# Block transposes for the softmax maxima, and two quads of heads in one accumulator, in a decode kernel that reads a KV cache

## The chip, the cores and the metric

The kernel runs on one core of one Trainium2 chip. The metric is the device time of one execution in microseconds, the median of several runs. Before the change it is 721.58 us (3 runs, 721.48 to 721.66).

## The reference

One decode step for two batch rows: attention over a cache of 4096 keys with 32 heads, a GELU MLP, and a gate that mixes the two. All values are float32.

```python
x (2,1,576); k_cache, v_cache (2,32,4096,128); wq (576,4096); wo (4096,576); w1 (576,4608); w2 (4608,576)
g = sigmoid((x * gate_w).sum(-1, keepdims=True))
q = (x @ wq) as (2,32,1,128)
p = softmax(einsum("bhqd,bhkd->bhqk", q, k_cache) * 128**-0.5)
a = einsum("bhqk,bhkd->bhqd", p, v_cache) reshaped to (2,1,4096) @ wo
b = gelu(x @ w1 + b1) @ w2 + b2
out = g * a + (1 - g) * b
```

## The kernel before

**Loads.** One large tile, `ring`, has three slots of 128 x 16384 numbers (8.39 MB). SyncE's queue fills them in a fixed order: first wq and w1, then K and V of 16 quads (a quad is four heads of one batch row: head e has partitions 32e to 32e+31, 128 keys each), and at last, in three loads, w2 and wo. `load_next` issues the next load into a slot as soon as what was in it has been used. The last load holds wo's rows 16 to 31, in pieces that get smaller (16-23, 23-27, 27-30, 30-31, then row 31 in three parts).

**One quad.** VectorE multiplies K by q in place (`mul`, L508), GpSimd adds two halves of a part of it (L512), VectorE sums (`red`, L513 and L514) into 128 scores a partition. `max_p` (L518) takes each partition's maximum. `max_t` (L523) is a TensorE matmul: the 128 maxima, broadcast to 128 columns, against a diagonal matrix `idsc` that holds the softmax scale, so that PSUM has all maxima in every row. `max_n` (L527) takes the negated maximum of each head's 32 columns. `softmax` (L533) runs four exponentials on ScalarE into `p`, one for each head, with the sums in `rs`. `av` (L544) multiplies p, 32 columns at a time, with V: each group of 16 columns (4 heads x 4 key blocks) is followed by the next group's 16, so half of the 32 rows that come out are of no use. `keep` (L556) masks the accumulator on VectorE, and `combine` (L562) adds the useful rows into the accumulator `oall`.

**Order.** The order on every engine is that of the program, written by hand. In iteration i of the loop over quads stand `max_n` and `softmax` of quad i-1, `mul` and `red` of quad i, `av` of quad i-1, `max_p` and `max_t` of quad i, then `keep` and `combine` of quad i-1. Every fourth iteration `q_unit` makes the next four quads' q.

**The end.** After the last K, `mlp_out(0, 24)` multiplies w2's first rows (L369 is the matmul of all rows that go to the accumulator `acc`, two to a row, and each of float32 is done in two passes), then come the last `av`, `keep`, `combine`, the normalisation (`norm_sum`, `norm_t`, `o_turn`) between further w2 rows, and `wo_out(0, FOLD)`. `last_out` copies `acc` with ScalarE (L448), takes the rows of wo from FOLD on into a second accumulator `res` (L459, four matmuls to a row, L483 for part of row 31), adds the copy with a fold matmul (L469) behind row FOLD + 3, copies `res` out of PSUM (L479, L488) and writes the result (L489).

Of the kernel before, what the change touches and what calls it, by code (L numbers as in the profile page):

```python
# [8 lines left out]
F32 = mybir.dt.float32  # L9
AF = mybir.ActivationFunctionType  # L10
ALU = mybir.AluOpType
AX = mybir.AxisListType
P = 128
# [6 lines left out]
def kernel(  # L20
# [14 lines left out]
    nc = tc.nc  # L35
# [6 lines left out]
    E = 4  # L42
    N = B * H // E
    PE_ = P // E
    R = E * SK // P
    RB = 512 // DH
    NT = R // RB
# [15 lines left out]
    SCALE = float(DH) ** -0.5  # L63
# [4 lines left out]
        (("w2", 28, 36), ("wx", 0, 1), ("wo", 0, 8), ("wo", 8, 16)),  # L68
        (("wo", 16, 23), ("wo", 23, 27), ("wo", 27, 30), ("wo", 30, 31), ("wo", 31, 32)),
    )  # L70
    FOLD = 23
    SLOT = R * DH
    ALIGN = 512
    FREE0 = 16512
# [5 lines left out]
    rp = ctx.enter_context(tc.tile_pool(name="rp", bufs=1))  # L80
    cp = ctx.enter_context(tc.tile_pool(name="cp", bufs=1))
    qm = ctx.enter_context(tc.tile_pool(name="qm", bufs=1))
    qp = ctx.enter_context(tc.tile_pool(name="qp", bufs=2))
    sp = ctx.enter_context(tc.tile_pool(name="sp", bufs=2))
    ep = ctx.enter_context(tc.tile_pool(name="ep", bufs=1))
    ps_acc = ctx.enter_context(tc.tile_pool(name="ps_acc", bufs=1, space=bass.MemoryType.PSUM))
    ps_av = ctx.enter_context(tc.tile_pool(name="ps_av", bufs=2, space=bass.MemoryType.PSUM))
    ps_big = ctx.enter_context(tc.tile_pool(name="ps_big", bufs=1, space=bass.MemoryType.PSUM))
    ps_o = ctx.enter_context(tc.tile_pool(name="ps_o", bufs=1, space=bass.MemoryType.PSUM))
    ps_sm = ctx.enter_context(tc.tile_pool(name="ps_sm", bufs=3, space=bass.MemoryType.PSUM))  # L90
# [80 lines left out]
    def temp(n, parts=P):  # L171
        t = ring[:parts, used["t"]:used["t"] + n]
        used["t"] += n
        assert used["t"] <= SLOTS * SLOT
        return t

    def late(n, parts=P):
        t = ring[:parts, used["e"]:used["e"] + n]
        used["e"] += n
        assert not seq and used["e"] <= used["z"]  # L180
        return t
# [18 lines left out]
    def load_next(what):  # L200

        free.add(what)
        while seq and held[-SLOTS] in free:
            load()
# [24 lines left out]
    ident = cp.tile([P, P], F32, name="ident")  # L229
    make_identity(nc, ident)  # L230
    ones = cp.tile([P, 1], F32, name="ones")
    nc.gpsimd.memset(ones, 1.0)
    idsc = cp.tile([P, P], F32, name="idsc")
    nc.scalar.mul(idsc, ident, SCALE)


    NPB = 1
    NQ = 4
    EB = E * RB
    NO = N * E  # L240
    pt = []
    for j in range(NPB):
        t = cp.tile([P, NT * EB + 32 - EB], F32, name=f"p{j}")
        nc.gpsimd.memset(t, 0.0)
        pt.append(t)
    rs = cp.tile([P, NO], F32, name="rs")
    nc.gpsimd.memset(rs, 0.0)


    sel = ident.rearrange("p (j c) -> p j c", j=4)[:, :, :EB].rearrange("p j (e r) -> p j e r", e=E)  # L250
    selr = cp.tile([P, RB], F32, name="selr")
    nc.vector.tensor_reduce(selr, sel.rearrange("p j e r -> p r j e"), AX.XY, ALU.add)
    pick = cp.tile([P, 2 * NO - E], F32, name="pick")
    nc.vector.memset(pick, 0.0)
    nc.vector.tensor_reduce(pick[:, NO - E:NO], sel.rearrange("p j e r -> p e j r"), AX.XY, ALU.add)

# [69 lines left out]
    qps2 = ps_sm.tile([NO, DH], F32, tag="sm", name="qps2")  # L328
    for f in range(HG):
        nc.tensor.matmul(qps2, to[:, f], qrow[:, f * DH:(f + 1) * DH], start=(f == 0), stop=(f == HG - 1))  # L330
    qall = cp.tile([NO, DH], F32, name="qall")
    nc.scalar.copy(qall, qps2)  # L332


    mine = cp.tile([NO, N], F32, name="mine")
# [64 lines left out]
    t = temp(NF * B).rearrange("p (r b) -> p r b", b=B)  # L400
# [18 lines left out]
    def mlp_x():  # L419
        for s in range(XS):  # L420
            acc_mm(hx[:, s], rows["wx"][:, s], s, lo=1)
# [23 lines left out]
    def last_out():  # L445
        res = ps_big.tile([32 * (NC - 1) + B, DO], F32, tag="big", name="res")
        sums = late(DS)
        nc.scalar.copy(sums, acc)  # L448

        def half(t, s):  # L450
            if s < 2:
                return t[:, s * DO:(s + 1) * DO]
            return t.rearrange("p (q g c) -> p g q c", q=2, g=2)[:, s - 2]

        def cols(row, s):
            return half(row[:, s // 2 * DS:(s // 2 + 1) * DS], s)

        def part(r, s):
            nc.tensor.matmul(  # L459
                res[32 * s:32 * s + B], oP[:, :, r], cols(rows["wo", r], s),  # L460
                start=r == FOLD, stop=r == 31, skip_group_check=True,
            )

        for r in range(FOLD, 31):
            for s in range(NC):
                part(r, s)
            if r == FOLD + 3:
                for s in range(NC):
                    nc.tensor.matmul(  # L469
                        res[32 * s:32 * s + B], fold[:, s // 2], half(sums, s),  # L470
                        start=False, stop=False, skip_group_check=True,
                    )

        osb = late(D, B)
        cpy = (nc.vector.tensor_copy, nc.scalar.copy)
        for s in range(2):
            part(31, s)
        for s in range(2):
            cpy[s](osb[:, s * DO:(s + 1) * DO], res[32 * s:32 * s + B])  # L479
        DW = DO // 2  # L480
        for q in range(2):
            for s in range(2, NC):
                nc.tensor.matmul(  # L483
                    res[32 * s:32 * s + B, q * DW:(q + 1) * DW], oP[:, :, 31], cols(rows["wo", 31], s)[:, q],
                    start=False, stop=True, skip_group_check=True,
                )
        for s in range(2, NC):
            cpy[s - 2](cols(osb, s), res[32 * s:32 * s + B].rearrange("p (q c) -> p q c", q=2))  # L488
        nc.sync.dma_start(out.rearrange("b s d -> (b s) d"), osb)  # L489


    st, mx, mt, bias, avs = {}, {}, {}, {}, {}
    oT = cp.tile([P, B, H], F32, name="oT")

    oall = ps_o.tile([NO, 512], F32, name="oall")
# [11 lines left out]
    def mul(i):  # L507
        nc.vector.tensor_mul(kt[i], kt[i], qs[i].unsqueeze(1).to_broadcast([P, R, DH]))  # L508

    def red(i):  # L510
        t = kt[i][:, :HALVED]
        nc.gpsimd.tensor_add(t[:, :, :DH2], t[:, :, :DH2], t[:, :, DH2:])  # L512
        nc.vector.tensor_reduce(st[i][:, HALVED:], kt[i][:, HALVED:], AX.X, ALU.add)  # L513
        nc.vector.tensor_reduce(st[i][:, :HALVED], t[:, :, :DH2], AX.X, ALU.add)  # L514

    def max_p(i):
        mx[i] = sp.tile([P, 1], F32, tag="m", name=f"m{i}")
        nc.vector.tensor_reduce(mx[i], st[i], AX.X, ALU.max)  # L518


    def max_t(i):
        mt[i] = ps_sm.tile([P, P], F32, tag="sm", name=f"mt{i}")
        nc.tensor.matmul(mt[i], mx[i].to_broadcast([P, P]), idsc, start=True, stop=True)  # L523

    def max_n(i):
        bias[i] = sp.tile([P, E], F32, tag="bs", name=f"bs{i}")
        nc.vector.tensor_reduce(bias[i], mt[i].rearrange("o (e p) -> o e p", e=E), AX.X, ALU.max, negate=True)  # L527

    def softmax(i):
        p = pt[i % NPB][:, :NT * EB].rearrange("p (t c) -> p t c", c=EB)  # L530
        for e in range(E):
            w = slice(e * PE_, (e + 1) * PE_)
            nc.scalar.activation(  # L533
                p[w, :, e * RB:(e + 1) * RB], st[i][w].rearrange("p (t c) -> p t c", c=RB), AF.Exp,
                bias=bias[i][w, e:e + 1], scale=SCALE, accum_out=rs[w, i * E + e:i * E + e + 1],
            )


    def av(i):
        ps = ps_av.tile([P, 512], F32, tag="av", name=f"av{i}")  # L540
        p = pt[i % NPB]
        for t in range(NT):
            j = t % 4
            nc.tensor.matmul(  # L544
                ps[32 * j:32 * j + 32],
                p[:, EB * t:EB * t + 32],
                vt[i][:, RB * t:RB * (t + 1)].rearrange("p r d -> p (r d)"),
                start=(t < 4),
                stop=(t >= NT - 4),
            )  # L550
        avs[i] = ps


    def keep(i):
        t = ep.tile([P, RB, DH], F32, tag="avs", name=f"avs{i}")
        nc.vector.tensor_mul(  # L556
            t, avs[i].rearrange("p (r d) -> p r d", d=DH), selr.unsqueeze(2).to_broadcast([P, RB, DH])
        )
        avs[i] = t

    def combine(i):
        nc.tensor.matmul(  # L562
            oall, pick[:, NO - E - i * E:2 * NO - E - i * E], avs[i].rearrange("p r d -> p (r d)"),
            start=(i == 0), stop=(i == N - 1), skip_group_check=True,
        )


# [16 lines left out]
    for i in range(N):  # L584
        k = i - 1
        if 0 <= k:
            max_n(k)
            softmax(k)
        st[i] = sp.tile([P, R], F32, tag="s", name=f"s{i}")
        mul(i)  # L590
        red(i)
        if 0 <= k:
            av(k)
            load_next(("v", k))
        if (i + 1) % NQ == 0 and i + 1 < N:
            q_unit((i + 1) // NQ)
        load_next(("k", i))
        max_p(i)
        max_t(i)
        if 0 <= k:  # L600
            keep(k)
            combine(k)

    k = N - 1
    max_n(k)
    softmax(k)
    mlp_out(0, 24)
    av(k)
    load_next(("v", k))
    assert not seq  # L610
    keep(k)
    combine(k)
    turn = late(P)
    nc.vector.tensor_copy(turn.rearrange("p (h k) -> p k h", k=KB), ident.rearrange("p (k h) -> p k h", k=KB))
    osum = late(DH, NO)
# [6 lines left out]
    mlp_x()  # L622
    wo_out(0, FOLD)
    last_out()


# [26 lines left out]
```

## Time and profile before

| | |
|---|---|
| median of the runs | 721.58 us |
| span of the profiled execution, first to last instruction | 719.8 us |
| time of that execution outside its span | not shown; the median is 1.8 us above the span |
| read from HBM | 308.59 MB |
| instructions | 3981, of them 1695 matmuls and 1695 weight loads on TensorE |
| busy: TensorE, VectorE, ScalarE, GpSimd | 237.2, 516.8, 38.3, 143.8 us |
| granted TensorE clock, mean over the span | 0.663 |

How to read it: PE is TensorE's matmuls, PEld its weight loads, DVE VectorE, ACT ScalarE, POOL GpSimd, SP SyncE; a name with q (SPq) is that engine's sequencer. A row of a group gives line, engine, operation, output <- inputs, shapes, count, then busy time and the mean in ns of one, and then the idle time of the engine just before, with what ended it. A row in order of time starts with start and duration in us; where it merges several instructions the duration is from the first to the last or their busy time, and the idle time before is in brackets. L and a number is a line of the kernel.

### The profile page before, as it was taken

To read this page: it belongs to the slowest core of one execution; us is meant where nothing else is said; L and a number is where in the kernel's file an instruction comes from. 1 tells how busy PE (TensorE), PEld (TensorE's weight loads), DVE (VectorE), ACT (ScalarE), POOL (GpSimd) and SP (SyncE) were. 2 spreads that over 40 slices of the span, in tenths; PEclk is the share of its full clock that TensorE was granted. 3 is DMA by queue.
4 is the path that set the end of the run, shared out by engine and by line. 5 is a ranking of instruction groups with operands and counts; after the bars stand their busy time and mean duration, and the time that the engine had idled before them with its cause. 6 is when DMAs were issued, how large, how long until landed. Compare 5 with 4: busy or idle time off the path is not lost.

```text
span 719.8 us, 3981 instructions
## 1 busy us (share of the span) xinstructions
PE 237.2 (33%) x1695; PEld 72.1 (10%) x1695; DVE 516.8 (72%) x146; ACT 38.3 (5%) x143; POOL 143.8 (20%) x31
## 2 busy tenths in 40 slices
PE   0682022230516060504142140506060503224198
PEld 0330000010101010101010010101010101001033
DVE  0104969789695969596969879696969596978900
ACT  0010010100001010101010100101010101010000
POOL 1000130404050403022040404040503113040400
PEclk9986557575757565755757575757575665757589
DMA  9999999999999999999999999999999999999997
GB/s 409 412 443 431 433 441 419 455 416 448 426 444 427 426 438 430 437 430 441 434 433 433 437 427 437 426 437 434 441 430 444 427 437 422 433 441 431 418 425 307
DMA packets 7277, 308.84 MB, mean 429 GB/s; under 512 B 830, under 2 KB 1362, under 8 KB 1628
## 3 DMA queue, kind: packets, MB, share of 16 engines
q1 hardware_dynamic: 7204, 308.55, 99.2%
q8 instruction: 13, 0.21, 0.1%
q10 hardware_dynamic: 56, 0.05, 0.0%
q14 instruction: 4, 0.03, 0.0%
HBM read 308.59 MB, written 0.00 MB: 429 GB/s over the span
## 4 chain that ended last, share of the span: by engine, by line
DMA 46%; DVE 35%; PE 16%; issue 1%; ACT 1%; ACTq 0%; POOL 0%; DVEq 0%; SPq 0%; POOLq 0%
DMA ring<-in_A_k_cache_dram 41%; DVE ring L508 19%; DVE s L513 10%; PE av L544 8%; DVE s L514 5%; DMA ring<-in_A_wo_dram 3%; DMA ring<-in_gate_w_dram 3%; PE hps L305 2%; PE qps L305 2%; PE oall L562 1%; PE acc L369 1%; PE mt L523 1%; ACT p L533 1%; ACTq L218 0%; DVE m L518 0%
## 5 line engine op out<-in xcount | busy, mean ns | idle before, releaser
L508 DVE TENSOR_TENSOR ring<-ring,q 128x16384 f32<-128x16384 f32 x16 | 275.6, 17225 | 108.9 <-DMA ring<-in_A_k_cache_dram 108.9
L512 POOL TENSOR_TENSOR ring<-ring 128x3968 f32<-128x3968 f32 x16 | 137.0, 8564 | 494.3 <-DVE ring L508 494.3
L513 DVE TENSOR_REDUCE s<-ring 128x66 f32<-128x8448 f32 x16 | 143.2, 8953 | 1.3
L544 PE MATMUL av<-ring,p 128*32 128x512 f32 x1024 | 133.7, 681 | 11.5 <-ACT p L533 6.2
L523 PE MATMUL mt<-idsc,m 128*128 128x128 f32 x32 | 12.6, 498 | 367.5 <-DVE m L518 367.5
L514 DVE TENSOR_REDUCE s<-ring 128x62 f32<-128x3968 f32 x16 | 68.4, 4276 | 0.0
L533 ACT ACTIVATE p<-s,bs 32x128 f32<-32x128 f32 x64 | 25.5, 398 | 487.8 <-DVE bs L527 486.6
L544 PEld LDWEIGHTS av<-ring,p 128*32 128x32 f32 x1024 | 35.6, 124 | 119.3 <-issue 102.4
L523 PEld LDWEIGHTS mt<-idsc,m 128*128 128x128 f32 x32 | 8.0, 310 | 383.2 <-DVE m L518 289.1
L353 PE MATMUL qb<-qm,spread 64*128 64x512 f32 x8 | 8.3, 1138 | 71.2 <-POOL qm L349 71.2
L562 PE MATMUL oall<-avs,pick 128*64 128x512 f32 x32 | 30.6, 1059 | 0.8 <-DVE avs L556 0.8
L556 DVE TENSOR_TENSOR avs<-av,selr 128x512 f32<-128x512 f32 x16 | 10.9, 680 | 16.1 <-PE av L544 16.1
L392 DVE TENSOR_TENSOR ring<-hps,ring 128x384 f32<-128x384 f32 x3 | 1.7, 558 | 27.2 <-PE hps L305 27.0
L263 DVE COPY ring<-ring 3x64 f32<-3x64 f32 x2 | 0.3, 180 | 19.8 <-DMA ring<-in_gate_w_dram 19.8
L349 POOL TENSOR_TENSOR qm<-qall,mine 64x512 f32<-64x512 f32 x4 | 4.1, 1032 | 38.4 <-ACT qall L332 38.4
L533 ACT ACTIVATION_READ_ACCUMULATOR p<-s,bs 32x1 f32 x64 | 11.8, 184 | 0.0
L369 PE MATMUL acc<-ring,hg 128*2 128x288 f32 x142 | 11.6, 456 | 0.0
L305 PE MATMUL hps<-ring 128*32 128x384 f32 x120 | 11.5, 549 | 0.0
L305 PE MATMUL qps<-ring 128*32 128x512 f32 x80 | 11.4, 737 | 0.0
L353 PEld LDWEIGHTS qb<-qm,spread 64*128 64x128 f32 x8 | 2.0, 307 | 74.2 <-POOL qm L349 74.2
L479 DVE COPY ring<-res 2x144 f32<-2x144 f32 x1 | 0.3, 298 | 12.6 <-PE res L483 12.6
L272 PE MATMUL xps<-ident,ring 3*128 3x3 f32 x10 | 1.3, 250 | 23.1 <-DMA ring<-in_gate_w_dram 23.1
(89 smaller groups left out, 75.3 us busy)
## 6 DMA issues: line engine op xcount, KB each, us to landing
ring<-in_B_w_dram SPq DMA_DIRECT2D x2, 4608.0 KB, 34.4
ring<-in_B_w_dram SPq DMA_DIRECT2D x2, 4032.0 KB
ring<-in_A_wo_dram SPq DMA_DIRECT2D x2, 2304.0 KB, 15.0
ring<-in_B_w_dram SPq DMA_DIRECT2D x1, 2160.0 KB
ring<-in_A_wo_dram SPq DMA_DIRECT2D x1, 2016.0 KB
ring<-in_B_w_dram SPq DMA_DIRECT2D x1, 1152.0 KB, 14.7
ring<-in_A_wo_dram SPq DMA_DIRECT2D x1, 1152.0 KB
ring<-in_A_wq_dram SPq DMA_DIRECT2D x1, 1024.0 KB
```

The lines of the kernel that those rows point to most:

```text
L305: nc.tensor.matmul(ps[32 * j:32 * j + 32, :width], lhs, ts[c][:, o:o + width], start=(k == 0), stop=last, skip_group_check=True,)
L353: nc.tensor.matmul(ps, spread, t.rearrange("p u d -> p (u d)"), start=True, stop=True)
L369: nc.tensor.matmul(acc[o:o + m], lhsT, rhs[:, (s - lo) * DS:(s - lo + 1) * DS], start=start, stop=stop, skip_group_check=True)
L508: nc.vector.tensor_mul(kt[i], kt[i], qs[i].unsqueeze(1).to_broadcast([P, R, DH]))
L512: nc.gpsimd.tensor_add(t[:, :, :DH2], t[:, :, :DH2], t[:, :, DH2:])
L513: nc.vector.tensor_reduce(st[i][:, HALVED:], kt[i][:, HALVED:], AX.X, ALU.add)
L514: nc.vector.tensor_reduce(st[i][:, :HALVED], t[:, :, :DH2], AX.X, ALU.add)
L523: nc.tensor.matmul(mt[i], mx[i].to_broadcast([P, P]), idsc, start=True, stop=True)
L533: nc.scalar.activation(p[w, :, e * RB:(e + 1) * RB], st[i][w].rearrange("p (t c) -> p t c", c=RB), AF.Exp, bias=bias[i][w, e:e + 1], scale ...
L544: nc.tensor.matmul(ps[32 * j:32 * j + 32], p[:, EB * t:EB * t + 32], vt[i][:, RB * t:RB * (t + 1)].rearrange("p r d -> p (r d)"), start=(t ...
L556: nc.vector.tensor_mul(t, avs[i].rearrange("p (r d) -> p r d", d=DH), selr.unsqueeze(2).to_broadcast([P, RB, DH]))
L562: nc.tensor.matmul(oall, pick[:, NO - E - i * E:2 * NO - E - i * E], avs[i].rearrange("p r d -> p (r d)"), start=(i == 0), stop=(i == N - ...
```

## The change

The parts of the edit:

- `max_t` becomes a VectorE transpose of 32 x 32 blocks of the broadcast maxima (32 columns instead of 128), so each head's partitions hold their own head's maxima; `max_n` then reduces 32 columns to one bias, right behind it in the same iteration and no longer at the start of the next. `idsc` is gone: the scale is multiplied into `qall`, and the exponential has no scale.
- `p` has 32 columns for each step, of which 16 are zero, with 16 more zeros ahead of the first. Even quads read 16 + 16 zero columns, odd quads 16 zero + 16 columns, so `av` of two successive quads accumulates in one PSUM bank (even quads in rows 0 to 15 of each 32, odd ones in rows 16 to 31). `keep` and `combine` run once for two quads; the masks `selr` and `pick` are made for 8 groups instead of 4.
- The q tile has one buffer instead of two.
- FOLD is 27 instead of 23, and the fold matmul stands behind row FOLD.

```diff
-    FOLD = 23
+    FOLD = 27
...
-    qp = ctx.enter_context(tc.tile_pool(name="qp", bufs=2))
+    qp = ctx.enter_context(tc.tile_pool(name="qp", bufs=1))
...
-    idsc = cp.tile([P, P], F32, name="idsc")
-    nc.scalar.mul(idsc, ident, SCALE)
...
-        t = cp.tile([P, NT * EB + 32 - EB], F32, name=f"p{j}")
+        t = cp.tile([P, NT * 32 + EB], F32, name=f"p{j}")
...
-    nc.scalar.copy(qall, qps2)
+    nc.scalar.mul(qall, qps2, SCALE)
...
-            if r == FOLD + 3:
+            if r == FOLD:
...
     def max_t(i):
-        mt[i] = ps_sm.tile([P, P], F32, tag="sm", name=f"mt{i}")
-        nc.tensor.matmul(mt[i], mx[i].to_broadcast([P, P]), idsc, start=True, stop=True)
+        mt[i] = sp.tile([P, PE_], F32, tag="mt", name=f"mt{i}")
+        nc.vector.transpose(mt[i], mx[i].to_broadcast([P, PE_]))
 
     def max_n(i):
-        bias[i] = sp.tile([P, E], F32, tag="bs", name=f"bs{i}")
-        nc.vector.tensor_reduce(bias[i], mt[i].rearrange("o (e p) -> o e p", e=E), AX.X, ALU.max, negate=True)
+        bias[i] = sp.tile([P, 1], F32, tag="bs", name=f"bs{i}")
+        nc.vector.tensor_reduce(bias[i], mt[i], AX.X, ALU.max, negate=True)
...
     def av(i):
-        ps = ps_av.tile([P, 512], F32, tag="av", name=f"av{i}")
+        half = i % 2
+        if half == 0:
+            avs[i // 2] = ps_av.tile([P, 512], F32, tag="av", name=f"av{i // 2}")
+        ps = avs[i // 2]
...
-                p[:, EB * t:EB * t + 32],
+                p[:, 32 * t + EB * (1 - half):32 * t + EB * (1 - half) + 32],
...
-                start=(t < 4),
-                stop=(t >= NT - 4),
+                start=(half == 0 and t < 4),
+                stop=(half == 1 and t >= NT - 4),
...
         if 0 <= k:
-            max_n(k)
             softmax(k)
...
         max_p(i)
         max_t(i)
-        if 0 <= k:
-            keep(k)
-            combine(k)
+        max_n(i)
+        if 0 <= k and k % 2:
+            keep(k // 2)
+            combine(k // 2)
 
     k = N - 1
-    max_n(k)
     softmax(k)
     mlp_out(0, 24)
     av(k)
     load_next(("v", k))
-    keep(k)
-    combine(k)
+    keep(k // 2)
+    combine(k // 2)
```

More of the change, by code (lines that the diff above doesn't have):

```diff
@@ L247 @@
     nc.gpsimd.memset(rs, 0.0)
-    sel = ident.rearrange("p (j c) -> p j c", j=4)[:, :, :EB].rearrange("p j (e r) -> p j e r", e=E)
+    G = 32 // RB
+    sel = ident.rearrange("p (j e r) -> p j e r", j=4, e=G)
     selr = cp.tile([P, RB], F32, name="selr")
     nc.vector.tensor_reduce(selr, sel.rearrange("p j e r -> p r j e"), AX.XY, ALU.add)
-    pick = cp.tile([P, 2 * NO - E], F32, name="pick")
+    pick = cp.tile([P, 2 * NO - G], F32, name="pick")
     nc.vector.memset(pick, 0.0)
-    nc.vector.tensor_reduce(pick[:, NO - E:NO], sel.rearrange("p j e r -> p e j r"), AX.XY, ALU.add)
+    nc.vector.tensor_reduce(pick[:, NO - G:NO], sel.rearrange("p j e r -> p e j r"), AX.XY, ALU.add)
     xe = temp(2 * P, B + 1).rearrange("p (e c) -> p e c", e=2)
@@ L521, in max_t @@
     def max_t(i):
-        mt[i] = ps_sm.tile([P, P], F32, tag="sm", name=f"mt{i}")
-        nc.tensor.matmul(mt[i], mx[i].to_broadcast([P, P]), idsc, start=True, stop=True)
+        mt[i] = sp.tile([P, PE_], F32, tag="mt", name=f"mt{i}")
+        nc.vector.transpose(mt[i], mx[i].to_broadcast([P, PE_]))
     def max_n(i):
-        bias[i] = sp.tile([P, E], F32, tag="bs", name=f"bs{i}")
-        nc.vector.tensor_reduce(bias[i], mt[i].rearrange("o (e p) -> o e p", e=E), AX.X, ALU.max, negate=True)
+        bias[i] = sp.tile([P, 1], F32, tag="bs", name=f"bs{i}")
+        nc.vector.tensor_reduce(bias[i], mt[i], AX.X, ALU.max, negate=True)
     def softmax(i):
-        p = pt[i % NPB][:, :NT * EB].rearrange("p (t c) -> p t c", c=EB)
+        p = pt[i % NPB][:, EB:].rearrange("p (t c) -> p t c", c=32)
         for e in range(E):
@@ L534, in softmax @@
                 p[w, :, e * RB:(e + 1) * RB], st[i][w].rearrange("p (t c) -> p t c", c=RB), AF.Exp,
-                bias=bias[i][w, e:e + 1], scale=SCALE, accum_out=rs[w, i * E + e:i * E + e + 1],
+                bias=bias[i][w], accum_out=rs[w, i * E + e:i * E + e + 1],
             )
     def av(i):
-        ps = ps_av.tile([P, 512], F32, tag="av", name=f"av{i}")
+        half = i % 2
+        if half == 0:
+            avs[i // 2] = ps_av.tile([P, 512], F32, tag="av", name=f"av{i // 2}")
+        ps = avs[i // 2]
         p = pt[i % NPB]
@@ L545, in av @@
                 ps[32 * j:32 * j + 32],
-                p[:, EB * t:EB * t + 32],
+                p[:, 32 * t + EB * (1 - half):32 * t + EB * (1 - half) + 32],
                 vt[i][:, RB * t:RB * (t + 1)].rearrange("p r d -> p (r d)"),
-                start=(t < 4),
-                stop=(t >= NT - 4),
+                start=(half == 0 and t < 4),
+                stop=(half == 1 and t >= NT - 4),
             )
-        avs[i] = ps
     def keep(i):
@@ L562, in combine @@
         nc.tensor.matmul(
-            oall, pick[:, NO - E - i * E:2 * NO - E - i * E], avs[i].rearrange("p r d -> p (r d)"),
-            start=(i == 0), stop=(i == N - 1), skip_group_check=True,
+            oall, pick[:, NO - G - i * G:2 * NO - G - i * G], avs[i].rearrange("p r d -> p (r d)"),
+            start=(i == 0), stop=(i == N // 2 - 1), skip_group_check=True,
         )
```

## The prediction

> **What bounds the kernel now.** I read the page's slices and queues first, then the chain that ended last, then the queues of one stretch in the middle, and last the order of time around one quad of heads and in the final 40 us.
>
> ```profile
> PE 237.2 (33%) x1695; PEld 72.1 (10%) x1695; DVE 516.8 (72%) x146; ACT 38.3 (5%) x143; POOL 143.8 (20%) x31
> DMA  9999999999999999999999999999999999999997
> q1 hardware_dynamic: 7204, 308.55, 99.2%
> q8 instruction: 13, 0.21, 0.1%
> HBM read 308.59 MB, written 0.00 MB: 429 GB/s over the span
> DMA 46%; DVE 35%; PE 16%; issue 1%; ACT 1%; ACTq 0%; POOL 0%; DVEq 0%; SPq 0%; POOLq 0%
> ```
>
> No engine is busy for more than 72%, but the DMA engines stand at nine tenths or more in all slices but the last, and q1 alone takes 99.2% of 16 engines. The chain (46% DMA, 35% VectorE) looks as if VectorE shared the bound. It does not: the chain goes back from a K load to the instruction that let it be issued, and counts as "DMA" or "DVE" time in which other loads were moving. The middle of the run alone says it:
>
> ```profile
> DMA packets 3816, 221.32 MB, mean 434 GB/s; under 512 B 431, under 2 KB 431, under 8 KB 431
> q1 hardware_dynamic: 3806, 221.19, 100.1%
> ```
>
> From 140 to 650 us the queue is full at 434 GB/s. All 308.59 MB at that rate are 711.0 us; the other 8.8 us of the 719.8 us span are the start, and the end, where transfers get small. An edit can move the time only if it starves the queue, adds or removes traffic, or lengthens what follows the last byte.
>
> How far is the queue from starving? One quad of heads in order of time:
>
> ```profile
> 139.22 0.33 SPq L130 DMA_DIRECT2D ring<-in_A_v_cache_dram  x1
> 139.22 0.29 DVE L518 TENSOR_REDUCE m<-s 128x1 f32<-128x128 f32 x1
> 139.66 0.77 PE L523 MATMUL mt<-idsc,m 128*128 128x128 f32 x2 [26.79 <-DVE m L518]
> 140.46 0.29 DVE L527 TENSOR_REDUCE bs<-mt 128x4 f32<-128x128 f32 x1 [0.35 <-PE mt L523]
> 142.98 7.99 PE L544 MATMUL av<-ring,p 128*32 128x512 f32 x64 [0.65 <-issue]
> 147.38 17.23 DVE L508 TENSOR_TENSOR ring<-ring,q 128x16384 f32<-128x16384 f32 x1 [6.63 <-DMA ring<-in_A_k_cache_dram]
> 151.03 0.33 SPq L130 DMA_DIRECT2D ring<-in_A_k_cache_dram  x1
> ```
>
> V is issued at 139.22, when the score reductions free a K slot, and the K load ahead of it lands only at 147.38: 8.2 us in hand. The next K is issued at 151.03, when the V product ends, while V (8.39 MB, 19.3 us at 434 GB/s) moves until 166.7: 15.7 us in hand. VectorE itself waits 6.63 us for K. So whatever a quad's small steps gain or lose, a few microseconds either way, ends in these waits.
>
> **The change, part by part.** The groups that it touches:
>
> ```profile
> L523 PE MATMUL mt<-idsc,m 128*128 128x128 f32 x32 | 12.6, 498 | 367.5 <-DVE m L518 367.5
> L562 PE MATMUL oall<-avs,pick 128*64 128x512 f32 x32 | 30.6, 1059 | 0.8 <-DVE avs L556 0.8
> L556 DVE TENSOR_TENSOR avs<-av,selr 128x512 f32<-128x512 f32 x16 | 10.9, 680 | 16.1 <-PE av L544 16.1
> L435 DVE STREAM_TRANSPOSE ring<-oT 128x32 f32<-128x32 f32 x2 | 0.3, 192 | 0.0
> ```
>
> *Maxima.* 16 matrix products leave TensorE (32 matmuls and as many weight loads); VectorE gets 16 transposes of 128x32. The nearest row, L435, is 0.192 us. With a broadcast source none is in the trace: bounds 0.15 us and, from the 128-wide reduction, 0.29 us; I take 0.19, the same shape. The maximum over 32 columns instead of 128 costs between that and today's 0.29. From the end of the scores to the bias: now 139.22 to 140.75, 1.53 us; then 0.29 + 0.19 + 0.19 = 0.67. The softmax and V product start some 0.9 us earlier; the V slot was 15.7 us ahead already. Worth 0.
>
> *Two quads in one accumulator.* 8 of 16 L556 products (8 x 0.680 = 5.4 us of VectorE) and 8 of 16 combines (32 instructions) go. The V product keeps its 1024 matmuls and its weights of 32 columns. None of it lies on a DMA wait; worth 0. The exponentials' output only gets a wider stride. If that doubled ACT's two microseconds per quad, 13 us of the V slot's lead would be left.
>
> *One q buffer.* The copy of the next four quads' q now waits for the product (L508) of the fourth quad, which ends before GpSimd makes that q's operand, and the next product waits for its K anyway. 0, at most the tenths that a late copy could take from VectorE's 6.63 us.
>
> *Scale moved into q; the scaled identity gone.* A copy becomes a multiplication of the same size; one 0.3 us instruction leaves ACT's idle start. The table load ahead of it (1.3 us) then stands before the gate's exponential, where the long q projection covers it. 0.
>
> *The last accumulator from row 27.* Rows 23 to 26 of wo go to the first accumulator: 4 x 4 matmuls in place of 4 x 8. Here, and only here, TensorE stands beside the end:
>
> ```profile
> 684.47 7.67 PE L369 MATMUL acc<-ring,hg 128*2 128x288 f32 x96
> 687.31 0.15 PEld L369 LDWEIGHTS acc<-ring,hg 128*2 128x2 f32 x4 [0.33 <-issue]
> 687.70 1.31 PEld L369 LDWEIGHTS acc<-ring,hg 128*2 128x2 f32 x24 [0.25 <-issue]
> 689.53 2.05 PEld L369 LDWEIGHTS acc<-ring,hg 128*2 128x2 f32 x40 [0.53 <-DMA ring<-in_B_w_dram]
> 707.19 5.99 PE L369 MATMUL acc<-ring,oP 128*2 128x288 f32 x92
> 713.17 0.84 PEld L459 LDWEIGHTS res<-ring,oP 128*2 128x2 f32 x32 [0.56 <-DMA ring<-in_A_wo_dram]
> 713.22 0.40 ACT L448 COPY ring<-acc 128x288 f32<-128x288 f32 x1 [28.13 <-PE acc L369]
> 714.03 0.23 PEld L469 LDWEIGHTS res<-ring,fold 128*2 128x2 f32 x8
> 715.28 0.84 PEld L459 LDWEIGHTS res<-ring,oP 128*2 128x2 f32 x32 [1.02 <-DMA ring<-in_A_wo_dram]
> 716.57 0.10 PEld L459 LDWEIGHTS res<-ring,oP 128*2 128x2 f32 x4 [0.44 <-DMA ring<-in_A_wo_dram]
> ```
>
> Three waits on wo: 0.56 us before row 23, 1.02 before row 27, 0.44 before row 31. Rows 23 to 26 at the L369 rate (5.99/92 = 0.065 us) take 1.04 us, to 714.21; ACT's copy, now after them, ends near 714.65, ahead of 715.28. The fold's 8 matmuls (0.23 us) then fall behind row 27, and 716.13 becomes 716.36: still ahead of 716.57. So 0, with 0.2 us in hand; without that wait, 0.23.
>
> *Fewer instructions to fetch.* q8 moves code: 0.1% of 16 engines for 13 packets, so about 0.9 us of one engine for each. Near the end:
>
> ```profile
> DMA  9999999997979897789494755556554343100000
> q8 instruction: 1, 0.02, 1.2%
> ```
>
> Between 712 and 717 us (40 slices of 0.125 us) one packet takes 1.2% of 16 x 5 us = 0.96 us of one engine, among engines that finish one after another between 714.4 and 716.5. 32+16+16 matmuls with their weight loads are 128 instructions, half a packet (2 x 1695 by the page's first line, over 13, is 261 a packet), so the last packet may go or slide behind the data. Bounds: 0, if another engine ends last, and -0.96. In the slices from 715.75 on still 4, 3, 4, 3, 1 tenths of the engines work, so several end within half a microsecond; I take -0.15. The Trainium skill ("Runtime: NRT & Kernel Launch", Instruction fetch mechanics) tells of refills in blocks of 16 KiB (0.21 MB over 13 agrees) and calls a crossing one DMA tail-bump, mostly hidden. By that this term is 0; the row above differs where the DMA engines are full.
>
> **TensorE's clock in the end is what could go wrong.** Now TensorE is woken at 681.85 by the maxima and the combine; without both (the last pair is combined later) it goes from the 15th V product straight to the w2 rows.
>
> ```profile
> 651.00 17.24 DVE ring L508
> ring<-in_B_w_dram SPq DMA_DIRECT2D x2, 4032.0 KB
> 679.60:681.85 2.25, 0.00 (x1) 0.00 (x1) 2.21 (x3) 0.00 (x0) 0.00 (x0) 0.50 0.96 416
> 684.40:687.70 3.30, 3.30 (x30) 0.99 (x32) 0.00 (x0) 0.67 (x4) 0.00 (x0) 0.52 0.88 376
> 687.70:689.50 1.80, 1.80 (x32) 0.57 (x24) 0.00 (x0) 0.00 (x0) 0.00 (x0) 1.00 0.98 420
> ```
>
> (After five busy columns come the granted clock, the DMA share and GB/s.) The last K landed at 651.00, V 19.3 us later, the first 14 rows of w2 (4.13 MB) 9.5 us after that, near 679.8. Their 56 matmuls can start there instead of 684.47. At half clock one takes 0.48/4 = 0.12 us, at full clock 1.31/24 = 0.055; the clock came 3.2 us after the w2 rows began, 5.85 after 681.85. So they are done between 684.5 and 686.5, and TensorE stands idle 3 to 5 us until the second half lands at 689.53. Today it is at full clock there, and 40 matmuls take 2.05 us. If the clock has gone down in that gap, a half-clock stretch of w us costs w x (1 - 0.051/0.12) = 0.57w: 1.8 us for 3.2, 3.2 us for 5.85 (its end in the V product). TensorE then runs unbroken to 712.61 (713.17 less the wait), so rows 23 to 26 shift to 712.61 + d for a loss d; plus 1.04, 0.45 for the copy, 0.23 fold and 0.64 for rows 28 to 30 (24 x 0.84/32), row 31 could start at 714.97 + d against 716.57: the time grows by d - 1.6 above a loss of 1.6 us. That is 0.2 us at d = 1.8 and 1.6 at d = 3.2; 0 if the clock stays up. Mean of these, weighted to the short stretch, since the w2 rows alone brought the clock in 3.2 us: +0.45.
>
> **Sum.** 719.8 + 0 (quads) - 0.15 (code) + 0.45 (clock at the end) = 720.1 us of span. The median of the runs is 721.58, 1.8 us above the profiled span; the execution's own time beyond that span isn't shown, so I keep the 1.8: 721.9 us. What a measurement here can tell from no change is about 0.2%, 1.4 us.
>
> **Rivals.**
> 1. *TensorE starts the end cold and pays in full (slower).* Place: second half of the w2 rows and the start of the last V product. Price: d = 3.2 gives +1.6, so 723.2 us; 3.8, half clock for two thirds of the V product's start as well, 723.8. It decides beyond a loss of 3.0 us, where the end is 1.4 later. For it: the clock column at 0.50 after each idle stretch, and 5.85 us from the first instruction to full clock. Against it: 3.2 us counted from the w2 rows. The Trainium skill states such a gate in "TensorE: Matmul & The Clock Gate", Part 1: half clock after an idle window of about 3.4 us, full after a busy one, the windows running free. The trace agrees as to the half clock. By that rule a gap of 3 to 5 us need not hold an idle window, and the loss changes from run to run.
> 2. *The last engine is freed by more than I take (faster).* If the removed packet sat on the one engine that ended last and the others end well before, -0.96: 720.6; with all engines ending as early as the first, near 714.4, -2.0: 719.6. Against it stand the 3 to 4 tenths around 716.
> 3. *The change removes nothing that counts*: the clock stays up, another engine ends last, 721.6 us. For it: the full queue. It differs from my forecast by its small term alone.
>
> **How the numbers follow.** My forecast (with rival 3) within 0.2%: 0.87. Rival 1 beyond 1.4 us: 0.09. Rival 2 beyond 1.4 us: 0.04. The range goes from 721.0 (part of the code term, clock up) to 723.0 (a cold stretch of about 5.5 us).
>
> **What would show it.** Right: DMA at nine tenths as now, the K landings where they are within a microsecond, VectorE waiting some 7 us for each K, one or no q8 packet fewer, the maxima's path at about 0.7 us, and the three waits on wo at the end still there or shortened. The clock term shows in the w2 rows: 40 weight loads from about 689.5 in 2 us or in 4 to 5, and a wait on wo before row 27 that has shrunk or gone. Wrong: a K product that waits for q or a copy, a V load issued later than its predecessor's landing, an added code packet on a late engine, or row 31's matmuls starting well after its landing.

## The result, and the profile after

The changed kernel takes 722.98 us (median of 9 runs, 722.80 to 724.27) against 721.61 before (9 runs, 721.45 to 721.73): the ratio over all runs is 1.0023, 95% interval 1.0014 to 1.0032 (the two medians alone give 1.0019). It is 1.4 us slower; I had forecast 721.9. The runs scatter more than before: six lie between 722.80 and 723.08 and three between 724.13 and 724.27. The profiled execution is one of the three (724.13, span 722.1), so its losses are larger than the median's: the spans of the nine runs have a median of 721.0.

From the page of the changed kernel (span; DMA share of the 40 slices; the two queues that move code, with packets, MB and share):

```profile
span 722.1 us, 3850 instructions
DMA  9999999999999999999999999999999999999996
q8 instruction: 13, 0.21, 0.1%
q14 instruction: 3, 0.02, 0.0%
```

The transfers are as full as before, and 128 TensorE instructions fewer have saved no packet on q8. On q14 one packet is missing; before the change there were four:

```profile
q14 instruction: 4, 0.03, 0.0%
```

One quad of the changed kernel in order of time, the same quad as in the prediction:

```profile
139.19 0.33 SPq L130 DMA_DIRECT2D ring<-in_A_v_cache_dram  x1
139.19 0.29 DVE L516 TENSOR_REDUCE m<-s 128x1 f32<-128x128 f32 x1
139.51 0.21 DVE L521 STREAM_TRANSPOSE mt<-m 128x32 f32<-128x32 f32 x1
139.76 0.19 DVE L525 TENSOR_REDUCE bs<-mt 128x1 f32<-128x32 f32 x1
142.19 8.80 PE L545 MATMUL av<-ring,p 128*32 128x512 f32 x64 [29.31 <-ACT p L531]
147.42 17.23 DVE L506 TENSOR_TENSOR ring<-ring,q 128x16384 f32<-128x16384 f32 x1 [7.48 <-DMA ring<-in_A_k_cache_dram]
151.05 0.33 SPq L130 DMA_DIRECT2D ring<-in_A_k_cache_dram  x1
```

All of this but the longer V product is as forecast. The bias is there at 139.95 instead of 140.75, the V product starts 0.8 us earlier and takes 0.8 us longer (the granted clock is 0.50 at its start in both traces, and the full clock comes 3.5 us into it, at 145.7, where before it came after 1.9 us, at 144.9), and the next K is issued at 151.05, against 151.03. K lands at 147.42 against 147.38 before.

The time is lost behind the stream of quads. The end of the changed kernel in order of time:

```profile
679.99 6.05 PE L367 MATMUL acc<-ring,hg 128*2 128x288 f32 x56 [26.15 <-DMA ring<-in_B_w_dram]
689.50 4.98 PE L367 MATMUL acc<-ring,hg 128*2 128x288 f32 x40 [3.46 <-DMA ring<-in_B_w_dram]
694.25 7.55 PE L545 MATMUL av<-ring,p 128*32 128x512 f32 x64
701.88 0.69 DVE L556 TENSOR_TENSOR avs<-av,selr 128x512 f32<-128x512 f32 x1 [19.79 <-PE av L545]
709.99 6.72 PE L367 MATMUL acc<-ring,oP 128*2 128x288 f32 x106
716.99 0.40 ACT L446 COPY ring<-acc 128x288 f32<-128x288 f32 x1 [32.76 <-PE acc L367]
717.44 0.11 PEld L467 LDWEIGHTS res<-ring,fold 128*2 128x2 f32 x8 [0.57 <-ACT ring L446]
719.56 0.29 SPq L487 DMA_DIRECT2D out_dram<-ring  x1
```

The first 56 matmuls of w2 start at 679.99, on the landing; then TensorE waits 3.46 us, and the next 40 take 4.98 us. The stretches with the granted clock (last three columns: clock, DMA share, GB/s) show why:

```profile
685.00:688.40 3.40, 1.04 (x16) 0.19 (x8) 0.00 (x0) 0.00 (x0) 0.00 (x0) 0.99 0.94 402
688.40:689.50 1.10, 0.01 (x1) 0.01 (x2) 0.00 (x0) 0.00 (x0) 0.00 (x0) 0.52 0.99 424
689.50:694.50 5.00, 5.00 (x44) 1.66 (x48) 0.00 (x0) 0.00 (x0) 0.00 (x0) 0.50 1.03 434
```

The full clock was there for 3.4 us, in which TensorE worked 1.04, and was gone about 1 us before the second half of w2 landed (688.45 in the clock's records). The V product and VectorE's masking of the last accumulator before the change:

```profile
691.96 7.05 PE L544 MATMUL av<-ring,p 128*32 128x512 f32 x64
699.08 0.69 DVE L556 TENSOR_TENSOR avs<-av,selr 128x512 f32<-128x512 f32 x1 [16.11 <-PE av L544]
```

The masking now starts at 701.88 and not at 699.08: TensorE is d = 2.80 us late (2.3 from the 40 matmuls, 0.5 from the start of the V product). None of the three waits on wo is left. In their place the fold waits 0.57 us for ScalarE's copy, and the result's write is issued at 719.56. Before:

```profile
717.71 0.28 SPq L489 DMA_DIRECT2D out_dram<-ring  x1
```

That is 1.85 us. The rest is behind it: from the issue of the write to the end of the span are 2.09 us before (719.80 - 717.71) and 2.57 after. 1.85 + 0.48 are the 2.33 us between the spans. The 0.48 us lie on GpSimd. These are its closing steps in the records of both traces (start in us, duration in ns):

```
before                                    after
719.23   17  EVENT_SEMAPHORE              721.08   17  EVENT_SEMAPHORE
719.31   78  DRAIN                        721.49  222  DRAIN
719.41   96  EVENT_SEMAPHORE_RANGE_CLEAR  721.74   96  EVENT_SEMAPHORE_RANGE_CLEAR
```

The drain starts 0.41 us after the step before it instead of 0.08, and takes longer, and the other engines wait for it. GpSimd's stream has 73 recorded instructions instead of 79, all six of the difference being semaphore instructions.

### The profile page after: what moved, and what is told of

The parts are those of the page before. It is cut to its first block, busy times and chain, and to the rows that moved or that the text cites. A ratio compares the mean times of both kernels' runs of the same rounds, so it can differ in the third digit from the quotient of the medians.

```text
span 722.1 us, 3850 instructions
## 1 busy us (share of the span) xinstructions
PE 212.6 (29%) x1631; PEld 61.3 (8%) x1631; DVE 513.9 (71%) x154; ACT 38.0 (5%) x142; POOL 144.2 (20%) x31
## 4 chain that ended last, share of the span: by engine, by line
DMA 46%; DVE 35%; PE 17%; issue 1%; ACT 0%; ACTq 0%; POOL 0%; DVEq 0%; SPq 0%; POOLq 0%
DMA ring<-in_A_k_cache_dram 38%; DVE ring L506 19%; PE av L545 10%; DVE s L511 10%; DMA ring<-in_B_w_dram 5%; DVE s L512 5%; DMA ring<-in_gate_w_dram 3%; PE acc L367 2%; PE oall L562 2%; PE qps L303 1%; DMA ring<-in_B_b_dram 1%; DVE avs L556 1%; ACT p L531 0%; DVE m L516 0%; PE zps L279 0%
## 5 line engine op out<-in xcount | busy, mean ns | idle before, releaser
L545 PE MATMUL av<-ring,p 128*32 128x512 f32 x1024 | 136.9, 695 | 175.6 <-ACT p L531 175.6
L562 PE MATMUL oall<-avs,pick 128*64 128x512 f32 x16 | 14.9, 1029 | 198.2 <-DVE avs L556 169.8
L367 PE MATMUL acc<-ring,hg 128*2 128x288 f32 x142 | 14.9, 564 | 29.6 <-DMA ring<-in_B_w_dram 29.6
L562 PEld LDWEIGHTS oall<-avs,pick 128*64 128x64 f32 x16 | 2.2, 196 | 205.4 <-DVE avs L556 205.4
L556 DVE TENSOR_TENSOR avs<-av,selr 128x512 f32<-128x512 f32 x8 | 5.5, 682 | 19.8 <-PE av L545 19.8
L353 ACT COPY q<-qb 128x512 f32<-128x512 f32 x4 | 2.3, 586 | 105.4 <-PE qb L351 105.4
```

The source lines that it names most:

```text
L367: nc.tensor.matmul(acc[o:o + m], lhsT, rhs[:, (s - lo) * DS:(s - lo + 1) * DS], start=start, stop=stop, skip_group_check=True)
L545: nc.tensor.matmul(ps[32 * j:32 * j + 32], p[:, 32 * t + EB * (1 - half):32 * t + EB * (1 - half) + 32], vt[i][:, RB * t:RB * (t + 1)].rea ...
L556: nc.vector.tensor_mul(t, avs[i].rearrange("p (r d) -> p r d", d=DH), selr.unsqueeze(2).to_broadcast([P, RB, DH]))
L562: nc.tensor.matmul(oall, pick[:, NO - G - i * G:2 * NO - G - i * G], avs[i].rearrange("p r d -> p (r d)"), start=(i == 0), stop=(i == N // ...
```

## The experiments

Three theories. **C**: the maxima and the 15th quad's combine, as the last things on TensorE ahead of w2, had held its rows back until 682 to 684 us; without them the rows start with the landing, are done early, and the gap until the second half takes the clock. **F**: the later FOLD puts the copy and the fold on the path. **I**: the code's packets fall elsewhere among the DMA engines. From the trace came a fourth, **G**: the closing steps on GpSimd.

**The parts alone.** Three kernels undo or isolate a part each.

```diff
 e2, on the kernel before
-    FOLD = 23
+    FOLD = 27
-            if r == FOLD + 3:
+            if r == FOLD:
```

> The kernel before with FOLD at 27 and nothing else. Theory C: TensorE is warm at 689.5 and in time, so 721.6 us within 0.3; the copy ends before row 27 lands. Theory F: the whole loss, 722.7 to 723. Theory I: 32 instructions fewer move the fetches a little, 721.4 to 722.

Measured: 721.70 us against 721.62 (ratio 1.0000, 0.9992 to 1.0009). With TensorE in time the later fold costs nothing measurable; theory F as the only cause is out.

```diff
 e3, on the kernel before: max_t, max_n, the scale and their places as in the change
-        nc.tensor.matmul(mt[i], mx[i].to_broadcast([P, P]), idsc, start=True, stop=True)
+        nc.vector.transpose(mt[i], mx[i].to_broadcast([P, PE_]))
```

> The kernel before with the maxima and their scale on VectorE, one accumulator a quad as before, FOLD 23. Theory C: the combine of the 15th quad still holds the w2 rows back until about 683 us, so TensorE gets its clock during them and has little idle time before 689.5: 721.6 us within 0.3, 40 matmuls in 2 to 3 us. Theory F: 721.6. Theory I: 64 instructions fewer, half of the loss, 722.2. If the transposes or the earlier bias themselves cost: 722.5 or more.

Measured: 721.80 us (1.0002, 0.9993 to 1.0011). The first w2 rows start later here than before the change, behind the combine:

```profile
685.07 0.11 PEld L367 LDWEIGHTS acc<-ring,hg 128*2 128x2 f32 x8 [1.61 <-issue]
```

```diff
 e4, on the kernel before: p, av, keep, combine, selr, pick and the one q buffer as in the change
-        if 0 <= k:
-            keep(k)
-            combine(k)
+        if 0 <= k and k % 2:
+            keep(k // 2)
+            combine(k // 2)
```

> The kernel before with two quads in one accumulator, the maxima on TensorE as before, FOLD 23. Theory C: the 16th quad's maxima (a TensorE matmul at about 681.8 us) still stand ahead of the w2 rows, which begin at about 682.6: their 56 matmuls end near 688 and TensorE is warm at 689.5: 721.6 us within 0.4. Theory F: 721.6. Theory I: 32 instructions fewer, 721.4 to 722.

Measured: 721.64 us (1.0001, 0.9992 to 1.0010). The w2 rows in order of time in e4:

```profile
682.62 6.24 PE L369 MATMUL acc<-ring,hg 128*2 128x288 f32 x56
689.52 2.61 PE L369 MATMUL acc<-ring,hg 128*2 128x288 f32 x40 [0.66 <-DMA ring<-in_B_w_dram]
```

One matmul of maxima ahead of them is enough: they start at 682.62, run until 688.86, TensorE waits 0.66 us and keeps its clock. Each part alone leaves one instruction that holds the rows back (the combine in e3, the maxima in e4); only both together take the last one away. No sum of the parts' costs would show it.

**The fold undone.**

```diff
 e1, on the changed kernel
-    FOLD = 27
+    FOLD = 23
-            if r == FOLD:
+            if r == FOLD + 3:
```

> The changed kernel with FOLD back at 23. Theory C (TensorE's clock is down when the second half of w2 lands, TensorE is late in the end): the 40 matmuls from about 689.5 us still take some 5 us, but ScalarE's copy and the fold no longer follow the late rows 23 to 26; TensorE's end comes about 1 us earlier than in the changed kernel: 721.8 to 722.3 us, still above 721.6. Theory F (the later fold alone is the cause): back at 721.6. Theory I (the code fetches on other DMA engines are the cause): 722.7 to 723, as the changed kernel.

Measured: 723.08 us (722.09 to 723.96; ratio 1.0020, 1.0011 to 1.0029). No gain over the changed kernel in the median, against theory C's expectation, and near where theory I had put it (that theory is answered at the code term, below). But the runs spread over 1.9 us, and the median cannot tell what FOLD does; the traces can (e9, below).

**TensorE kept warm, or its order changed.**

```diff
 e6, on the changed kernel
-    mlp_out(0, 24)
+    mlp_out(0, 14)
+    warm = ps_sm.tile([P, P], F32, tag="sm", name="warm")
+    for _ in range(WARM):    # WARM = 20
+        nc.tensor.matmul(warm, ident, ident, start=True, stop=True)
+    mlp_out(14, 24)
```

> The changed kernel with 20 products of the identity with itself between the two halves of the w2 rows, whose result nobody reads: TensorE is kept busy in the gap. Theory C: full clock at 689.5, 40 matmuls in 2 to 2.5 us, TensorE late by 0 to 1 us and row 31 waits for its landing again: 721.9 to 722.2 us. If the clock is not the cause, more work makes it no faster: 723 or more.

Measured: 722.37 us (722.24 to 723.26; 1.0013, 1.0004 to 1.0022). In order of time:

```profile
685.48 4.54 PEld L610 LDWEIGHTS warm<-ident 128*128 128x128 f32 x40 [0.49 <-issue]
690.15 2.05 PEld L368 LDWEIGHTS acc<-ring,hg 128*2 128x2 f32 x40
715.53 0.11 PEld L458 LDWEIGHTS res<-ring,oP 128*2 128x2 f32 x8 [1.34 <-DMA ring<-in_A_wo_dram]
717.90 0.29 SPq L488 DMA_DIRECT2D out_dram<-ring  x1
```

Work that nobody needs makes the kernel 0.6 us faster. The 40 loads take 2.05 us as before the change though they start 0.65 us late, row 27 waits for its landing again, and the write goes out at 717.90 instead of 719.56. That is theory C's cause itself: the edit does nothing but fill the idle time. From the write to the end are still 2.58 us, theory G's part; the median is 0.2 us above what I had expected.

```diff
 e5, on the changed kernel
-    mlp_out(0, 24)
     av(k)
     load_next(("v", k))
+    mlp_out(0, 24)
     keep(k // 2)
```

> The changed kernel with the last V product ahead of the 24 w2 rows on TensorE. Theory C (the idle gap before the second half of w2 takes TensorE's clock): no gap is left between w2's halves; the V product runs from about 684.2 to 694, the w2 rows after it at full clock until 699, TensorE reaches row 23 of wo before it lands: about 721.9 us, which is 721.6 and 0.3 to 0.5 for theory G. Theory G (GpSimd's closing instructions take some 0.4 us longer, because its stream has six instructions fewer and its code block ends there): stays, so not below 721.9. If the loss had another cause than TensorE's order: 723.

Measured: 722.30 us (722.09 to 722.82; 1.0011, 1.0002 to 1.0020), the write at 717.78. The V product, cold for its first 5.3 us, takes 9.69 us and then all 96 matmuls of w2 run at full clock. With the write 0.07 us from that of before, the kernel is still 0.7 us slower, 0.4 more than I had expected: 0.55 of it lies in the span (0.07 and theory G's 0.48), the rest outside it.

**GpSimd's closing steps.**

```diff
 e7, on the changed kernel
-    nc.gpsimd.memset(ones, 1.0)
+    for _ in range(9):
+        nc.gpsimd.memset(ones, 1.0)
```

> The changed kernel with eight more memsets of one column on GpSimd at the start. Theory G: the closing instructions on GpSimd run as before the change (the step after the last write 0.4 us shorter), so 722.5 us, 0.4 to 0.5 below the changed kernel; the cold w2 rows stay. Without theory G: 723.0, unchanged.

Measured: 722.66 us (721.89 to 723.40; 1.0015, 1.0006 to 1.0024). In order of time, and its span:

```profile
689.46 4.98 PE L368 MATMUL acc<-ring,hg 128*2 128x288 f32 x40 [3.86 <-DMA ring<-in_B_w_dram]
719.14 0.28 SPq L488 DMA_DIRECT2D out_dram<-ring  x1
```

```profile
span 721.2 us, 3858 instructions
```

The rows are as cold as in the changed kernel (4.98 us), but from the write to the end are 2.09 us again (721.23 by the records), and q14 has its fourth packet back. Eight useless memsets at the start shorten the end by 0.48 us; the median falls by 0.3, within the scatter of both kernels.

```diff
 e8, on the changed kernel, with e7's memsets
+    gate = ps_sm.tile([P, P], F32, tag="sm", name="gate")
+    nc.tensor.matmul(gate, mx[k].to_broadcast([P, P]), ident, start=True, stop=True)
     mlp_out(0, 24)
```

> The changed kernel with one TensorE product of the 16th quad's maxima with the identity ahead of the w2 rows (its result is not read), and the eight memsets of e7. Theory C: the rows start at about 681.9 and not at 679.9, have little gap before 689.5, TensorE is warm there: together with theory G 721.6 us. Theory C alone: 722.0. If neither holds: 723.

Measured: 721.90 us against 721.56 (1.0005, 0.9996 to 1.0014).

```profile
682.04 0.80 PE L608 MATMUL gate<-ident,m 128*128 128x128 f32 x2 [26.60 <-DVE m L517]
682.76 6.08 PE L368 MATMUL acc<-ring,hg 128*2 128x288 f32 x56
689.79 2.61 PE L368 MATMUL acc<-ring,hg 128*2 128x288 f32 x40 [0.94 <-DMA ring<-in_B_w_dram]
717.83 0.29 SPq L488 DMA_DIRECT2D out_dram<-ring  x1
```

One matmul put back, whose result is not read, and the eight memsets, and all but 0.3 us of the loss is gone; the rest is within the interval. Ten of the eleven runs lie between 721.73 and 722.03. Of the 0.3, 0.1 is in the span (719.9 us, 719.8 before) and 0.2 outside it.

```diff
 e10, on the kernel before: b1r, ones, p, rs and to
-        nc.gpsimd.memset(t, 0.0)
+        nc.vector.memset(t, 0.0)
```

> The kernel before with five early memsets moved from GpSimd to VectorE, nothing else. Theory G (a step at a fixed place of GpSimd's instruction stream, which fewer instructions push into the closing steps): the closing steps on GpSimd grow by 0.4 to 0.5 us, 722.0 us. Without theory G, 721.6.

Measured: 722.17 us against 721.56 (1.0009, 1.0000 to 1.0018). The write is issued early, but the end is not:

```profile
717.52 0.28 SPq L489 DMA_DIRECT2D out_dram<-ring  x1
```

```profile
span 720.0 us, 3980 instructions
```

2.49 us by the records, q14 at three packets. Theory G's loss is made in the kernel before, without any of the change. Among all kernels here those with three q14 packets need 2.49 to 2.58 us behind the write and those with four 2.09 to 2.10, but for e3 (2.40), in which VectorE's own drain comes 0.37 us late and VectorE has the longest stream of all. The place is fixed, too: in the changed kernel, e1, e5, e6 and e10 alike the gap (0.39 to 0.42 us) stands ahead of the 69th recorded instruction of GpSimd's stream, in e10, whose stream is one longer, therefore one step earlier (718.96 to 719.37). In the other kernels that instruction comes long before the end. That the refill of the code is what holds the engine is suggested by this, not shown.

**Two more.** e9 is e1 with e7's memsets.

> The changed kernel with FOLD 23 and the eight memsets of e7: against e7 (FOLD 27, cold w2 rows, 722.66) it shows what the later fold costs when TensorE is late. If ScalarE's copy and the fold behind the late rows cost (wait of 0.57 us before the fold in the changed kernel): 0.4 to 0.8 us below e7, 721.9 to 722.3. If FOLD is neutral: 722.4 to 722.9, as e7. The wide run-to-run spread of 1 us and more stays in both cases, since the w2 rows are still cold in most runs.

Measured: 722.19 us (721.60 to 723.31; 1.0011, 1.0002 to 1.0020), 0.5 below e7. But e1 was 0.1 above the changed kernel, so the medians do not settle it. The traces of the four kernels with the cold gap do, for the profiled executions: each shows d and the delay of the write, and TensorE waits for no landing after the gap. With FOLD at 27 the write is 1.85 us later at d = 2.80 and 1.43 at 2.37 (e7); with FOLD at 23, 0.15 at 1.51 (e1) and 0.22 at 1.58 (e9). So TensorE had 0.95 us in hand with FOLD at 27, both times, and 1.36 with FOLD at 23, both times: the later fold costs 0.4 us once TensorE is more than 1.4 us late.

```diff
 e11, on the changed kernel, with e7's memsets
     softmax(k)
-    mlp_out(0, 24)
     av(k)
     load_next(("v", k))
     assert not seq
+    mlp_out(0, 14)
     keep(k // 2)
     combine(k // 2)
...
     norm_sum()
+    mlp_out(14, 24)
+    norm_t()
     mlp_out(24, 30)
-    norm_t()
-    mlp_out(30, 33)
     o_turn(turn)
-    mlp_out(33, NF)
+    mlp_out(30, NF)
```

> The changed kernel with the eight memsets, the last V product ahead of the w2 rows and the normalisation between them. Theory C and G: no cold rows after the gap, no longer closing steps, TensorE ahead of wo's landings: 721.6 to 721.9 us, the bound of the transfers, no better than before. If TensorE's order in the end still limited the kernel before: below 721.3.

Measured: 721.87 us (721.58 to 722.24; 1.0003, 0.9995 to 1.0012). This order of TensorE's work gives nothing more either. No version beat the kernel before, whose last row waits 0.44 us for its landing (716.57, in the prediction).

## Why the prediction failed

*The bound, the quads, the head.* Right. From 140 to 650 us the queue ran at 434 GB/s again, VectorE waits for K somewhat longer, the transpose takes 0.211 us (0.19 taken, bounds 0.15 and 0.29), and no part alone costs anything measurable.

*The mechanism at the end.* Named with its place: start at "near 679.8" (679.99), done "between 684.5 and 686.5" (686.04), idle 3 to 5 us (3.46). It was told as the slower rival with a chance of 0.09, and in the profiled execution that rival came.

*The failed step is the clock term of the sum, sized +0.45.* It was 1.85 us in the profiled execution and some 0.7 in an average one (below). The losses d in the four traces with a cold gap were 2.80 (after), 2.37 (e7), 1.58 (e9) and 1.51 (e1): they lie between the 1.8 and the 3.2 us of the prediction or just below, so the weight on the short stretch was no great error, nor was the formula (5.8 us cold would give 3.3, and cost 2.80). What was wrong is TensorE's slack of 1.6 us. It was 0.95 in both traces with FOLD at 27, so that the two cases cost 0.85 and 2.25 where I had 0.2 and 1.6. I had counted the slack from the end of the weight loads at 712.61 (the queue's wait of 0.56 us), whereas the copy waits for the last matmul, which ended at 713.18. That accounts for 0.57 of the 0.65; the copy itself, 716.99 to 717.44, took the 0.45 that I had. What the remaining 0.08 are is open.

*Two terms were missing.* The closing steps on GpSimd, which the prediction did not look at, cost 0.48 us. The change takes no instruction of the program away from GpSimd (its memset of p only gets longer, 0.54 to 0.97 us at the start); six semaphore instructions fell away, in e3 and e4 none, so it takes the parts together. Why, no run shows. And the prediction kept 1.8 us for the time outside the span: over the nine runs it is 2.0 on average, as in e1 and e4 to e11 (1.96 to 2.04), against 1.8 in the kernel before, e2 and e3 (1.80 to 1.84). What these 0.2 us are stays open; e10, which is the kernel before with five memsets moved, has them too.

*The account.* For the spans of the profiled executions it closes: 1.85 + 0.48 of 2.33. The median of 1.37 us is 1.2 in the spans (721.0 against 719.8) and 0.2 outside; of the 1.2, 0.48 are closing steps if they take as long in every run, and the remaining 0.7 are the clock's part, worked out by difference. So in an average run the two missing terms together were as large as the clock's. That the median still lies within the range, at its upper edge of 723.0, is luck: the range was made from the clock and the code alone. That a change of 1.4 us could not be told from none, as the prediction held, was too cautious: the interval reaches 0.09%, some 0.65 us, to each side.

*The code term, -0.15, was 0.* 13 packets, and the last of them moved behind the data (714.34 to 718.81), but the transfers end at the same time. The view from 712 to 717 us of the changed kernel:

```profile
DMA  9998998999979869687767765544533321100000
q8 instruction: 1, 0.02, 1.2%
```

The share falls to nothing in the same slice as before, at 716.4, and by the records the last packet of data ends at 716.50 in both: the other engines were as late, which the prediction gave as one of its bounds. With that theory I is out for the profiled execution.

*The clock's rule.* The prediction weighed "TensorE: Matmul & The Clock Gate" of the Trainium skill, Part 1, and left open whether a gap of 3 to 5 us would hold an idle window. Here it did not need a wholly idle one: the clock went down at 688.45 after a stretch of 3.4 us in which TensorE had worked for 1.04. That the windows run free agrees with the scatter: kernels with the cold gap spread by 1.5 to 1.9 us over their runs, e2, e3 and e4 without it by 0.25 to 0.40. It is no clean division: e5, e6, e8 and e11, without the cold gap too, spread by 0.7 to 1.0. So the rule would explain the spread; the runs other than the profiled ones have no trace that would show it.

## What to carry to other kernels

An instruction that is taken off an engine may have been the last one that made the next work start late, and late may have been right: look at what that engine does next, whether it now stands idle between two transfers, and at which clock it goes on. When parts of a change each hold back the same work, judge them together as well as one by one. Count a slack from the end of the work that the next step waits for, not from the wait of the queue ahead of it, and compare the steps behind the last write, too, where an engine that nobody touched can hold up the rest.

## What was unexpected of the hardware

GpSimd stood still for some 0.4 us between two closing steps once its stream had 73 or 74 recorded instructions instead of 79, always ahead of the 69th; eight one-column memsets at the start took this away (2.57 to 2.09 us behind the write), and five fewer in the kernel before made it (2.09 to 2.49). TensorE lost its full clock after 2.4 us of idle time (686.04 to 688.45), 1 us before its next matmul, and needed 5.8 us of work to have it back (689.50 to 695.27 in the clock's records). And 4.5 us of useless matmuls paid for themselves, since they kept the following 40 at 2.61 us instead of 4.98.
